# Gate logits of the last three token groups as TensorE products instead of sixteen VectorE multiply-and-sums

## The chip, the cores and the metric

The kernel runs on one core of a Trainium2 chip. The metric is device time in microseconds (us), the median of several executions of the same compiled kernel; lower is better. Engines are named as in the profile: PE (TensorE products), PEld (TensorE weight loads), DVE (VectorE), ACT (ScalarE), POOL (GpSimd), SP (the engine that only issues DMAs here).

## The reference

Three stages, in float32. A recurrent attention over 768 steps gives 3072 rows of 320 numbers. A dense two-layer network (320 to 2048 to 320, leaky ReLU) turns each row into a new row. Then every row is sent to one of eight experts:

```python
logits = x @ w_gate                          # 3072 x 320 by 320 x 8
expert_idx = np.argmax(logits, axis=1)
probs = softmax(logits)                      # gate_w = the chosen expert's probability
for e in range(E):
    mask = expert_idx == e
    out[mask] = gate_w[mask, None] * (np.maximum(x[mask] @ w1[e], 0.0) @ w2[e])
```

## The kernel before

**Groups.** The 3072 rows go in 12 groups of 256 (two tiles of 128 rows), numbered 0 to 11. Attention works chunk by chunk; as soon as a group's rows are there, the dense network runs on them in 16 pairs of *halves*: the odd half of pair f is `layer1(f)` (8 products into a `psH` bank, then ACT `g`, DVE `g`, ACT `gh`), the even half is `layer2(f-2)` (6 products that add up in the two `psX` banks) followed by `close` (POOL `gl`, line 712). `layer2` of a pair needs that pair's `gl`. A written-out list of words (START, STEP, LATE, END, TAIL) sets the order of everything; H is one half. In TAIL only the dense network and the first expert's loads are left; then `go` (line 1127) runs the expert slots j = 0 to 15, each in eight steps f of `layer1` (8 products) and, two steps late, `layer2` (6 products).

**Routing of a group.** With the last `layer2` of a group, `take` copies its rows from `psX` to `X` (one buffer, line 739, ACT). The list that `route` (line 723) returns is then worked off, one entry per half: 16 entries `logits` (line 742, DVE, one multiply-and-sum over 128 x 320 for one expert and one tile), `first` and `second` (argmax), `third` (line 760: position products on PE, DVE reciprocal), `fourth` (line 772: SP writes both tiles of `X` to the DRAM tensor `x2d`, line 774), `fifth` with `place(0)` and three entries later `place(1)` (line 787: POOL scatters row numbers into the DRAM tables `tbl[0]`, `tbl[1]`). That is 28 entries after `take`. The routing of group 9 begins in END, that of group 10 in TAIL, that of group 11 with TAIL's last half and goes on in `go`, where PACE gives the number of entries in each step f: (2, 1) in slot 0, (3, 3) in slot 1, (2, 2) later. Behind it in the same list come the entries of `plan.make`, which decide the later slots.

**What reads the routing's results.** Slots 0 to 2 are chosen early. Their row numbers are loaded by `fetch` (line 1031, SP, `sid` from `tbl[0]` and `tbl[1]`; the loads for slots 0 and 1 both stand at the word i of TAIL), and POOL gathers the rows from `x2d` with them (line 1039), at the words t. The framework orders accesses to one DRAM tensor as it does tiles: a gather from `x2d` waits for all earlier writes to it, a write waits for earlier gathers, a load from `tbl` waits for earlier scatters, and a scatter waits for earlier loads. SP, POOL and PE work strictly in order. SP's list also holds the expert weights' loads (`raw`, lines 1017 and 1019, five pieces per slot into one buffer; a piece waits until the old one has been split by ACT and by DVE, or by POOL for slot 1, lines 1059 to 1069).

**Order of TAIL around the change**, with the half's number: 337 to 341, first `raw` pieces, i (sid loads), 342 to 344, `memset`, ..., 350, first gather, ..., 356 (`take` of group 10), ..., 360, second gather, ..., 363, third gather, ..., 376, fourth gather, ..., 386 (`take` of group 11). Group 9's `take` is in half 324.

**Banks.** In END `s.bank()` gives one of four `psA` banks; in TAIL one of the two `psH` banks, which `layer1` also uses; in `go` `layer1` goes round these two and one more (`eph`).

Of the kernel before, what the change touches and what calls it, by code (L numbers as in the profile page):

```python
# [11 lines left out]
F32 = mybir.dt.float32  # L12
# [14 lines left out]
DM = H * D  # L27
FF = 2048
NF = FF // 128
E, F2 = 8, 1024  # L30
SL = 256
CAP = NT + SL
NSLOT = NT // SL + E - 1
PACE = (2, 1), (3, 3), (2, 2)
FETCH = 1, 5
EARLY, NE = {9: (0, 1), 10: (2,)}, 3
LOAD, SPLIT = 18, 27
# [34 lines left out]
def layouts(r, k, v, w, a, b, moe_w_in, moe_w_out, moe2_w_gate, moe2_w1, moe2_w2):  # L72


    def pair(x):
        return x.reshape(B, 2, 4, NC, C, D).transpose(3, 1, 5, 0, 2, 4).reshape(NC, 2, D, 16, C)

    def pad(y):
        return np.ascontiguousarray(np.concatenate([y, y[:, :, :24]], axis=2).reshape(NC, 128, -1))

    def flat(x):
        return np.ascontiguousarray(x.reshape(B, 2, 4, NC, C, D).transpose(3, 5, 1, 0, 2, 4).reshape(NC, D, NU * C))

    def words(x):
        x = np.ascontiguousarray(x)
        return x.view(np.int64) if x.dtype == np.float64 else x

    pw = pair(w)
    hw = pad(np.concatenate([np.zeros(pw.shape[:-1] + (1,), pw.dtype), pw], axis=-1))
    hw = np.concatenate([hw, np.zeros(hw.shape[:2] + (2,), hw.dtype)], axis=-1)  # L90
    w1 = moe2_w1
    tail = w1[:, 256:320]
    hw1 = np.concatenate([w1[:, 0:128], w1[:, 128:256], np.concatenate([tail, tail], axis=1)], axis=2)
    hw2 = moe2_w2.reshape(E, 8, 128, DM).transpose(0, 2, 1, 3).reshape(E, 128, 8 * DM)
    wt = moe_w_in[256:320]
    return {
        "nr": r, "nk": k, "nv": v, "nw": w, "na": a, "nb": b,
        "h1": np.ascontiguousarray(np.concatenate([hw, pad(pair(a)), pad(np.concatenate([pair(k), pair(b)], axis=-1))], axis=2)),
        "hr": flat(r),
        "hvt": flat(v),  # L100
        "hv": np.ascontiguousarray(v.reshape(B, 2, 4, NC, C, D).transpose(3, 4, 1, 0, 2, 5).reshape(NC, C, NU * D)),
        "hwi": words(np.concatenate([moe_w_in[0:128], moe_w_in[128:256], np.concatenate([wt[:, 0:FF // 2], wt[:, FF // 2:]], axis=0)], axis=1)),
        "hwo": words(moe_w_out.reshape(NF, 128, DM).transpose(1, 0, 2).reshape(128, NF * DM)),
        "hwg": np.ascontiguousarray(moe2_w_gate.T),
        "hwe": np.ascontiguousarray(np.concatenate([hw1, hw2], axis=2)),
    }

# [19 lines left out]
def place(n):  # L127

    return 16 * (n // 16) + 8 * (n % 2) + n % 16 // 2
# [371 lines left out]
class Moe1:  # L501
# [170 lines left out]
    def rows(s, g):  # L672

        x = s.x2d.rearrange("(b n) d -> b (n d)", b=B)[:, 2 * C * g * XW:]
        s.nc.sync.dma_start(x.rearrange("b (q f) -> q b f", q=120), s.wis[0:120, None, 0:616].bitcast(F32).to_broadcast([120, B, 616]))

    def load_x(s, src):
        nc = s.nc
        s.xr = s.p2.tile([128, 3, 256], F32R, name="xl", tag="xl")
        x = s.xr.bitcast(F32)  # L680
        nc.sync.dma_start(x[:, 0:2, :], src[0:256].rearrange("(k p) t -> p k t", p=128))
        nc.sync.dma_start(x[0:64, 2, :], src[256:320])
        nc.sync.dma_start(x[64:128, 2, :], src[256:320])
# [36 lines left out]
            for n, (x, w) in enumerate(((gh, s.woh), (gh, s.wol), (gl, s.woh))):  # L720
                nc.tensor.matmul(s.x2[t][:, 0:DM], x[:, o], w[:, f, :], start=(f == 0 and n == 0), stop=(f == NF - 1 and n == 2))  # L721

    def route(s, dest, ids):

        nc = s.nc
        X = s.r1.tile([128, 2, XW], F32, name="X2", tag="X2")
        lg = s.r2.tile([128, 2, E], F32, name="lg")
        sm = s.r2.tile([128, 2, 4], F32, name="sm")
        wk = s.r2.tile([128, 2, E], F32, name="wk")
        oh = s.r2.tile([128, 2, E], BF16, name="oh")  # L730
        dst = s.r2.tile([128, 2], I32, name="dst")
        bc = lambda x: x.to_broadcast([128, 2, E])
        code = s.code[:, None, :].to_broadcast([128, 2, E])
        box = {}
        x2 = s.x2

        def take():
            for t in range(2):
                nc.scalar.copy(out=X[:, t, 0:DM], in_=x2[t][:, 0:DM])  # L739

        def logits(e, t):
            nc.vector.scalar_tensor_tensor(  # L742
                out=s.junk, in0=X[:, t, 0:DM], scalar=1.0, in1=s.wg[:, e], op0=ALU.mult, op1=ALU.mult, accum_out=lg[:, t, e:e + 1])

        def rest():
            pass

        def first():
            nc.vector.tensor_reduce(out=sm[:, :, 0], in_=lg, axis=AX.X, op=ALU.max)
            nc.vector.tensor_tensor(out=wk, in0=lg, in1=bc(sm[:, :, 0:1]), op=ALU.is_equal)  # L750
            nc.vector.tensor_tensor(out=lg, in0=lg, in1=bc(sm[:, :, 0:1]), op=ALU.subtract)
            nc.scalar.activation(out=lg, in_=lg, func=AF.Exp)
            nc.scalar.copy(out=X[:, :, DM:DM + 64], in_=X[:, :, DM - 64:DM])

        def second():
            nc.vector.tensor_tensor(out=wk, in0=wk, in1=code, op=ALU.mult)
            nc.vector.tensor_reduce(out=sm[:, :, 1], in_=wk, axis=AX.X, op=ALU.max)
            nc.vector.tensor_tensor(out=oh, in0=code, in1=bc(sm[:, :, 1:2]), op=ALU.is_equal)

        def third():  # L760
            nc.vector.tensor_reduce(out=sm[:, :, 2], in_=lg, axis=AX.X, op=ALU.add)
            ps = box["ps"] = s.bank()
            for t in range(2):
                o = ps[:, E * t:E * t + E]
                nc.tensor.matmul(o, s.tri, oh[:, t, :], start=True, stop=False)
                if t:
                    nc.tensor.matmul(o, s.ones, oh[:, 0, :], start=False, stop=False)
                nc.tensor.matmul(o, s.ones, s.run, start=False, stop=True)
            nc.vector.tensor_scalar_add(out=sm[:, :, 2], in0=sm[:, :, 2], scalar1=1e-9)
            nc.vector.reciprocal(out=X[:, :, DM + 64], in_=sm[:, :, 2])  # L770

        def fourth():
            for t in range(2):
                nc.sync.dma_start(dest[t], X[:, t, :])
            nc.vector.tensor_tensor(
                out=wk, in0=box["ps"][:, 0:2 * E].rearrange("p (t e) -> p t e", t=2), in1=s.ecap[:, None, :].to_broadcast([128, 2, E]), op=ALU.add)
            nc.vector.tensor_tensor(out=wk, in0=wk, in1=oh, op=ALU.mult)
            nc.vector.tensor_reduce(out=sm[:, :, 3], in_=wk, axis=AX.X, op=ALU.add)
            nc.vector.tensor_copy(dst, sm[:, :, 3])

        def fifth():
            for t in range(2):
                nc.vector.tensor_tensor(out=s.run, in0=s.run, in1=oh[:, t, :], op=ALU.add)
            place(0)

        def place(t):
            nc.gpsimd.indirect_dma_start(
                out=s.tbl[t], out_offset=bass.IndirectOffsetOnAxis(ap=dst[:, t:t + 1], axis=0), in_=ids[:, t:t + 1], in_offset=None,
                bounds_check=NTB - 1, oob_is_err=False)

        return [take] + [lambda e=e, t=t: logits(e, t) for e in range(E) for t in range(2)] + [first, rest, second, rest, rest, rest, third, fourth, fifth, rest, rest, lambda: place(1)]

    def units(s):

        lag = []

        def second():
            g, f, gh, gl = lag.pop(0)
            s.layer2(f, gh, gl)
            if f == NF - 1:  # L800
                r = s.route([s.x2c[2 * g], s.x2c[2 * g + 1]], s.ids[:, 2 * g:2 * g + 2])
                r.pop(0)()
                return r
            return []

        for g in range(NC // 2):
            for f in range(NF):
                *a, close = s.layer1(f)
                lag.append((g, f, *a))
                yield []  # L810
                r = second() if len(lag) > 2 else []
                close()
                yield r
        while lag:
            yield second()
# [155 lines left out]
class Moe2:  # L971
# [155 lines left out]
    def go(s, ready, finish):  # L1127
# [3 lines left out]
        def step(n):  # L1131
            for _ in range(n):
                if ready:
                    ready.pop(0)()
                elif next(finish, True):
                    return False
            return True

        for j in range(NFIX):
            sp = s.split(j + 1, s.nc.gpsimd if j == 0 else None) if j + 1 < NFIX else []  # L1140
            ld = []
            for f in range(8):
                lag.append((j, f, *s.layer1(j, f)))
                if sp:
                    sp.pop(0)()
                step(PACE[min(j, 2)][0])
                if len(lag) > 2:
                    s.layer2(*lag.pop(0))
                if sp and f % 3 != 2:
                    sp.pop(0)()  # L1150
                step(PACE[min(j, 2)][1])
                if f == 1 and j + 2 < NFIX:
# [94 lines left out]
def overlap(tc, at, m1, plan):  # L1247

    nc = tc.nc
# [36 lines left out]
    def half():  # L1286
# [10 lines left out]
        if done == 2 * NF:  # L1297
            for _ in ws:
                pass
            m1.rows(9)  # L1300
        g = done // (2 * NF)
        new = next(units, None)
        if new is None:
# [116 lines left out]
```

## Time and profile before

| | us |
|---|---|
| median of 3 executions | 1122.68 (1119.37 to 1127.97) |
| the profiled execution's own time | 1121.85 |
| its span in the trace | 1120.1 |
| PE busy in the span | 953.4 (85%) |
| DVE busy in the span | 820.3 (73%) |

The time lies 1.75 us above the span, and the profiled execution 0.83 us below the median. Times in the text are us from the span's start. A busy share is a mean over stages: the table says nothing yet on which engine sets the end.

### The profile page before, as it was taken

The page shows a single profiled execution, that of the slowest core. Times are in us where ns is not written, and L with a number is a line of the kernel's source. Part 1 is how long each engine was busy: PE and PEld are TensorE (multiplying, and loading weights), DVE is VectorE, ACT ScalarE, POOL GpSimd, SP SyncE. Part 2 cuts the span into 40 slices and gives each one's busy share as a digit, 9 for nine tenths or more (in the row PEclk, how much of TensorE's full clock was granted, in tenths as well). Part 3 has the DMA queues.
Part 4 walks back from the last instruction along what each step waited for, and adds up shares of the span by engine and source line. Part 5 has one row for each costly group of instructions (what it writes and reads, how often), then busy time and mean ns, then how long its engine had stood idle before and what let it go on. Part 6 is the DMA issues. An engine that isn't in the chain of part 4 may idle for free. (4 is left out here: it accounts for less than half of the span.)

```text
span 1120.1 us, 40696 instructions
## 1 busy us (share of the span) xinstructions
PE 953.4 (85%) x16817; PEld 897.7 (80%) x16817; DVE 820.3 (73%) x1946; ACT 527.8 (47%) x1308; POOL 503.2 (45%) x690
## 2 busy tenths in 40 slices
PE   3476778978799899999899999999787799999993
PEld 3366676868788888888788888999777799999992
DVE  8989787757778777868786777676569677777760
ACT  4455454653344344444444344444444466666640
POOL 5123144215863498338843783334537123233220
PEclk9999986878999999999999999999898899999997
DMA  7878776855546654565645342334235653741620
GB/s 248 238 220 224 215 197 175 226 149 153 147 133 165 145 160 138 162 157 162 151 135 144 91 90 76 102 89 134 54 83 160 138 168 113 231 117 58 190 78 11
DMA packets 132379, 163.18 MB, mean 146 GB/s; under 512 B 67708, under 2 KB 89868, under 8 KB 132056
## 3 DMA queue, kind: packets, MB, share of 16 engines
q1 hardware_dynamic: 122071, 141.30, 46.7%
q10 hardware_dynamic: 5760, 10.49, 3.2%
q0 software_dynamic: 4352, 8.69, 2.6%
q8 instruction: 135, 2.21, 0.9%
q14 instruction: 61, 0.49, 0.2%
HBM read 127.61 MB, written 42.27 MB: 152 GB/s over the span
## 5 line engine op out<-in xcount | busy, mean ns | idle before, releaser
L712 POOL TENSOR_TENSOR gl<-g,gh 128x256 fp32r<-128x256 f32 x192 | 155.2, 811 | 224.5 <-ACT gh L711 194.2
L710 DVE TENSOR_TENSOR g<-psH,g 128x256 f32<-128x256 f32 x192 | 81.1, 423 | 117.1 <-ACT g L709 110.5
L711 ACT CAST gh<-g 128x256 fp32r<-128x256 f32 x192 | 77.9, 406 | 165.7 <-DVE g L710 158.1
L721 PE MATMUL psX<-woh,gl 128*128 128x320 f32 x384 | 125.1, 326 | 12.4 <-POOL gl L712 11.9
L721 PE MATMUL psX<-woh,gh 128*128 128x320 f32 x384 | 133.6, 348 | 1.2 <-ACT woh L638 1.1
L709 ACT ACTIVATE g<-psH 128x256 f32<-128x256 f32 x192 | 73.7, 384 | 119.5 <-PE psH L705 89.0
L721 PE MATMUL psX<-wol,gh 128*128 128x320 f32 x384 | 123.2, 321 | 0.2 <-issue 0.2
L742 DVE SCALAR_TENSOR_TENSOR junk<-X,raws 128x320 bf16<-128x320 f32 x192 | 113.6, 591 | 11.5 <-ACT X L739 9.0
L259 PE MATMUL psA<-AtI,KB 40*64 40x72 f32 x1408 | 72.1, 266 | 37.9 <-DVE KB L238 18.7
L259 PEld LDWEIGHTS psA<-AtI,KB 40*64 40x64 f32 x1408 | 63.9, 169 | 44.4 <-POOL woh L237 18.6
L1123 POOL DMA_INDIRECT out<-ey,sid x32 | 34.5, 1078 | 122.9 <-ACT ey L1122 63.2
L705 PE MATMUL psH<-xh,wih 128*128 128x256 f32 x384 | 86.8, 309 | 3.3 <-DVE g L710 2.9
L721 PEld LDWEIGHTS psX<-woh,gl 128*128 128x128 f32 x384 | 76.4, 199 | 15.8 <-POOL gl L712 15.7
L721 PEld LDWEIGHTS psX<-woh,gh 128*128 128x128 f32 x384 | 76.3, 199 | 7.3 <-ACT gh L711 1.5
L299 POOL TENSOR_TENSOR itmp<-Tinv 128x30 f32<-128x30 f32 (+14 forms) x120 | 69.9, 582 | 26.3 <-DVE Tinv L291 19.1
L705 PE MATMUL psH<-xl,wih 128*128 128x256 f32 x384 | 81.0, 294 | 0.3 <-DVE xl L690 0.3
L705 PE MATMUL psH<-xh,wil 128*128 128x256 f32 x384 | 80.5, 293 | 0.0
L721 PEld LDWEIGHTS psX<-wol,gh 128*128 128x128 f32 x384 | 76.6, 200 | 0.7 <-issue 0.4
L305 POOL TENSOR_TENSOR Tinv<-Tinv,itmp 128x30 f32<-128x30 f32 (+14 forms) x120 | 73.4, 611 | 7.8
L705 PEld LDWEIGHTS psH<-xh,wih 128*128 128x128 f32 x384 | 66.3, 200 | 8.3 <-DVE g L710 5.6
L705 PEld LDWEIGHTS psH<-xl,wih 128*128 128x128 f32 x384 | 63.3, 202 | 0.6 <-DVE xl L690 0.6
L1101 DVE SCALAR_TENSOR_TENSOR ehl<-psH,ehh 128x256 fp32r<-128x256 f32 x86 | 36.1, 420 | 37.7 <-ACT ehh L1100 34.9
(278 smaller groups left out, 2762.7 us busy)
## 6 DMA issues: line engine op xcount, KB each, us to landing
raw<-hwe SPq DMA_DIRECT2D x48, 512.0 KB
raw<-hwe SPq DMA_DIRECT2D x32, 640.0 KB
in<-h SPq DMA_DIRECT2D x23, 521.0 KB
KB<-h SPq DMA_DIRECT2D x22, 512.0 KB
L<-dKBr SPq DMA_DIRECT2D x24, 320.0 KB
dKBr<-KBr SPq DMA_DIRECT2D x22, 320.0 KB
lamY<-dl SPq DMA_DIRECT2D x24, 264.0 KB
dl<-lam SPq DMA_DIRECT2D x22, 264.0 KB
```

The costliest lines, as they stand in the source:

```text
L259: nc.tensor.matmul(v[64 * i:64 * i + 64, k, :], z["KB"][64 * i:64 * i + 40, p, :], z["AtI"][64 * i:64 * i + 40, p, :], start=True, stop=True)
L299: eng.tensor_tensor(out=box["v"], in0=T[:, k + 1:32, k:k + 1].to_broadcast([128, n, k]), in1=T[:, k:k + 1, 0:k].to_broadcast([128, n, k]), ...
L305: eng.tensor_tensor(out=T[:, k + 1:32, 0:k], in0=T[:, k + 1:32, 0:k], in1=box["v"], op=ALU.add)
L705: nc.tensor.matmul(ps[:, 0:256], w, x, start=(n == 0), stop=(n == 7))
L709: nc.scalar.activation(out=g, in_=ps[:, 0:256], func=AF.Copy, scale=0.01)
L710: nc.vector.tensor_tensor(out=g, in0=ps[:, 0:256], in1=g, op=ALU.max)
L711: nc.scalar.copy(out=gh, in_=g)
L712: return gh, gl, lambda: nc.gpsimd.tensor_tensor(out=gl, in0=g, in1=gh, op=ALU.subtract)
L721: nc.tensor.matmul(s.x2[t][:, 0:DM], x[:, o], w[:, f, :], start=(f == 0 and n == 0), stop=(f == NF - 1 and n == 2))
L742: nc.vector.scalar_tensor_tensor(out=s.junk, in0=X[:, t, 0:DM], scalar=1.0, in1=s.wg[:, e], op0=ALU.mult, op1=ALU.mult, accum_out=lg[:, t, ...
L1101: nc.vector.scalar_tensor_tensor(out=hl, in0=ps, scalar=0.0, in1=hh, op0=ALU.max, op1=ALU.subtract)
L1123: nc.gpsimd.indirect_dma_start(out=s.out, out_offset=bass.IndirectOffsetOnAxis(ap=ids[:, t:t + 1], axis=0), in_=y[:, t, :], in_offset=None ...
```

## The change

Groups 9, 10 and 11 get their logits otherwise. `turn(t)` transposes the three column blocks of a tile of `X` on PE (columns 0, 128 and 192 on; the rows of the gate's weights that would count twice are zero) into a bank, ACT copies them to SBUF; `product(t)` multiplies them with the gate's weights in three float32 products into eight columns of the same bank, and ACT copies these to `lg`. The six entries `turn`, `rest`, `product` for two tiles replace sixteen, and two more `rest` stand ahead of `third`: 20 entries in place of 28. `fourth` is entry 16 instead of 24, `fifth` 17 instead of 25, `place(1)` 20 instead of 28. A new load of the gate's weights stands behind `rows(9)` in SP's list, and slot 1's PACE is (2, 2).

```diff
-PACE = (2, 1), (3, 3), (2, 2)
+PACE = (2, 1), (2, 2), (2, 2)
+TURNED = 9
...
+    gate = np.zeros((128, 3, E), np.float32)
+    gate[:, 0], gate[:, 1], gate[64:, 2] = moe2_w_gate[0:128], moe2_w_gate[128:256], moe2_w_gate[256:320]
...
+    def late(s):
+
+        s.gate = s.none.bitcast(F32)[:, 0:3 * E].rearrange("p (n e) -> p n e", n=3)
+        s.nc.sync.dma_start(s.gate, s.i["hwt"])
+        s.wT = s.raws.bitcast(F32)[:, 0:2, 0:384]
...
+        def turn(t):
+            ps = box[t] = s.bank()
+            for n, a in enumerate((0, 128, DM - 128)):
+                nc.tensor.transpose(ps[:, 128 * n:128 * n + 128], X[:, t, a:a + 128], s.k.ident)
+            nc.scalar.copy(out=s.wT[:, t], in_=ps[:, 0:384])
+
+        def product(t):
+            o = box[t][:, 0:E]
+            for n in range(3):
+                nc.tensor.matmul(o, s.wT[:, t, 128 * n:128 * n + 128], s.gate[:, n, :], start=n == 0, stop=n == 2)
+            nc.scalar.copy(out=lg[:, t], in_=o)
...
-        return [take] + [lambda e=e, t=t: logits(e, t) for e in range(E) for t in range(2)] + [first, rest, second, rest, rest, rest, third, fourth, fifth, rest, rest, lambda: place(1)]
+        if turned:
+            by = [lambda: turn(0), rest, lambda: product(0), lambda: turn(1), rest, lambda: product(1)]
+        else:
+            by = [lambda e=e, t=t: logits(e, t) for e in range(E) for t in range(2)]
+        return [take] + by + [first, rest, second] + [rest] * (5 if turned else 3) + [third, fourth, fifth, rest, rest, lambda: place(1)]
...
             m1.rows(9)
+            m1.late()
```

## Rows read from the trace of the kernel before

**Rows 1.** Busy time by stage: stretch, length, busy us (instructions), granted clock, DMA share, GB/s.
```profile
750.00:800.00 50.00, 42.36 (x564) 39.89 (x552) 30.65 (x115) 20.95 (x54) 21.20 (x25) 0.94 0.39 105
800.00:850.00 50.00, 42.54 (x294) 39.42 (x293) 37.05 (x99) 24.66 (x58) 27.01 (x29) 0.96 0.37 92
850.00:900.00 50.00, 39.59 (x271) 38.83 (x270) 37.86 (x90) 21.09 (x46) 19.85 (x18) 0.86 0.58 130
900.00:950.00 50.00, 50.00 (x387) 49.98 (x386) 37.02 (x65) 31.60 (x66) 14.16 (x16) 1.00 0.50 149
```

**Rows 2.** PE's waits from 740 to 900: us in total, times, longest.
```profile
PE psX L721 <- POOL gl L712: 6.6, 2, 6.5
PE epy L1113 <- ACT ey L1122: 5.5, 1, 5.5
PE psH L765 <- DVE ehl L1101: 4.4, 1, 4.4
PE eph L1097 <- ACT X L739: 3.9, 1, 3.9
```

**Rows 3.** Timeline of all engines around group 9's take: start, us, what.
```profile
756.07 0.31 PE L721 MATMUL psX<-woh,gl 128*128 128x320 f32 x1
...
758.33 0.75 ACT L739 COPY X<-psX 128x320 f32<-128x320 f32 x2
```

**Rows 4.** POOL's timeline in TAIL; in brackets idle before and releaser.
```profile
774.83 1.02 POOL L712 TENSOR_TENSOR gl<-g,gh 128x256 fp32r<-128x256 f32 x1 [0.82 <-ACT gh L711]
...
794.60 1.04 POOL L1039 DMA_INDIRECT xg<-x2d,sid  x1 [6.53 <-issue]
...
815.43 0.74 POOL L712 TENSOR_TENSOR gl<-g,gh 128x256 fp32r<-128x256 f32 x1 [0.27 <-ACT gh L711]
...
822.96 1.01 POOL L1039 DMA_INDIRECT xg<-x2d,sid  x1
```

**Rows 5.** SP's timeline from 735 to 910, the issues of row numbers and of x2d.
```profile
776.34 2.52 SPq L1031 DMA_DIRECT2D sid<-tbl  x4
...
782.24 1.32 SPq L774 DMA_DIRECT2D x2d<-X  x2
...
826.21 1.14 SPq L774 DMA_DIRECT2D x2d<-X  x2
...
843.60 0.90 SPq L1031 DMA_DIRECT2D sid<-tbl  x2
```

**Rows 6.** PE's timeline at the end of its longest wait.
```profile
797.79 0.63 PE L721 MATMUL psX<-woh,gl 128*128 128x320 f32 x1 [6.46 <-POOL gl L712]
```

**Rows 7.** DMA issues from 740 to 900: engine, count, median us to landing where shown.
```profile
xg<-x2d,sid POOLq DMA_INDIRECT x10, 3.1
tbl<-ids,dst POOLq DMA_INDIRECT x8, 16.9
```

**Rows 8.** Cost of a transpose and of a float32 product: PE's timeline, two places.
```profile
765.30 1.42 PE L475 MATMUL psA<-Rr,L 104*40 104x32 f32 x64
...
827.90 0.82 PE L1080 MATMUL epx<-ident,xg 128*128 128x128 f32 x6
```

**Rows 9.** Line 742 from 830 to 860: ns min/median/max, first and last start.
```profile
L742 DVE SCALAR_TENSOR_TENSOR junk<-X,raws x16: 480/492/1464, 837.8 to 851.8; 128x320 bf16<-128x320 f32 x16
```

**Rows 10.** Timeline of all engines over the first expert slot.
```profile
831.47 0.31 PE L721 MATMUL psX<-woh,gl 128*128 128x320 f32 x1
...
837.36 0.76 ACT L739 COPY X<-psX 128x320 f32<-128x320 f32 x2 [5.96 <-DMA x2d<-X]
...
839.60 5.80 POOL L1060 TENSOR_TENSOR bl<-raw,bh 128x512 fp32r<-128x512 f32 x4 [8.73 <-ACT bh L1059]
...
857.70 0.17 PE L765 MATMUL psH<-oh,tri 128*128 128x8 bf16 x1 [4.36 <-DVE ehl L1101]
...
859.58 0.84 PE L1097 MATMUL eph<-bxh,bh 128*128 128x256 f32 x3
```

**Rows 11.** The same timeline where slot 1's rows go out.
```profile
881.56 0.98 POOL L1123 DMA_INDIRECT out<-ey,sid  x1 [15.05 <-DMA out<-ey,sid]
...
887.74 0.63 PE L1113 MATMUL epy<-ah,ehh 128*128 128x320 f32 x1 [5.47 <-ACT ey L1122]
```

More of the change, by code (lines that the diff above doesn't have):

```diff
@@ L104, in layouts @@
         "hwg": np.ascontiguousarray(moe2_w_gate.T),
+        "hwt": gate,
         "hwe": np.ascontiguousarray(np.concatenate([hw1, hw2], axis=2)),
@@ L721, in layer2, with route @@
                 nc.tensor.matmul(s.x2[t][:, 0:DM], x[:, o], w[:, f, :], start=(f == 0 and n == 0), stop=(f == NF - 1 and n == 2))
-    def route(s, dest, ids):
+    def route(s, dest, ids, turned=False):
         nc = s.nc
@@ L800, in second @@
             if f == NF - 1:
-                r = s.route([s.x2c[2 * g], s.x2c[2 * g + 1]], s.ids[:, 2 * g:2 * g + 2])
+                r = s.route([s.x2c[2 * g], s.x2c[2 * g + 1]], s.ids[:, 2 * g:2 * g + 2], g >= TURNED)
                 r.pop(0)()
```

## The prediction

> **What bounds the kernel now.** I read the stages first [rows 1]. From 900 on PE is busy all the time at full clock, 387 instructions in 50 us, 0.129 us each: there the end is set by products alone, and whatever PE loses or wins before 900 moves the end by as much. From 750 to 900 it is idle for 25.5 of 150 us, and all three routings that change lie there. The clock costs more: 800 to 850 has 294 instructions, 37.9 us at 0.129, for which it took 42.54; 850 to 900 has 271, 35.0 us, in 39.59. So 4.6 us are lost to the half clock in each. Second I read PE's waits there [rows 2]: four hold 20.4 us, for POOL, for the output rows, for DVE and for `X`. Last I followed each one to its release.
>
> The first ends at 797.79 after 6.46 us, so PE stopped at 791.33 [rows 6]. POOL stood at a gather from 788.07 to 794.60 [rows 4]; no releaser is shown, but the gather reads `x2d`, whose write was issued at 782.24 [rows 5], so that write took about 12.4 us. The second write, issued at 826.21 [rows 5], held ACT's `take` until 837.36 [rows 10], 11.1 us, and PE lost 3.9 [rows 2]. The third wait ends at 857.70 with the position products [rows 10]; the sixteen sums of line 742 fill DVE ahead of them from 837.8 to 851.8, up to 1464 ns each where POOL works beside them, against 492 [rows 9]. The fourth, 5.47, is slot 1's output buffer: its second scatter stood 15.05 us for the landing of the first [rows 11].
>
> **Part 1, group 9 in END (loss 4.0).** The sums here have cover: PE is nearly full, so their removal is worth nothing. `turn(0)` follows the last `layer2` on PE, which ends at 756.38, but needs the first copy of `X`, ready at about 758.7 [rows 3]: PE waits 2.3 us, with the next `layer1` and attention's transposes queued behind. Six transposes cost 0.82 [rows 8]. A float32 product runs as two passes; 64 passes with 40 weight columns took 1.42 [rows 8], 22 ns each, scaled to 128 columns 71 ns, so twelve cost 0.85; bounds 0.27 (unscaled) and 1.55 (0.129 each). Together 1.7 per group, an estimate, with no cover where PE is full. ACT's four small copies are covered: it is busy 21 to 25 us in 50 [rows 1]. The gate's load is one issue on SP eight groups earlier, under 0.7 us (half of an `x2d` pair [rows 5]), with attention's products as its cover; I take nothing. PACE (2, 2) leaves 44 entries for 24 places in slot 0 and 4 a step in slot 1, done by its fifth step as before: nothing.
>
> **Part 2, group 9's tables (loss 2.7).** Everything behind the logits comes eight halves earlier, and passes the word i. Before, the row-number loads of slots 0 and 1 stood ahead of group 9's scatters. Now `place(0)` (half 340) stands ahead of them and `place(1)` (half 343) behind: the loads wait for the first scatter to land, POOL waits for the loads, and `gl` of half 344 queues behind POOL. Meanwhile the old gather wait goes, since `x2d` is written early. `third` moves to half 338, whose close was at 774.83 [rows 4]: `x2d` goes at about 774.9 and lands 11.1 to 12.4 later, near 787. `place(0)` goes about 777.7 (one pair of halves, 14 products, 1.81 us, and the DVE steps). Its landing is between 3.1 us, a gather's, and 16.9, the one table write that shows it [rows 7]. I take 9.3: like the 16.9 it follows close behind an `x2d` write, and I let it land with that. That is 787.0. Four loads take 2.5 us to issue [rows 5] and the last some 2 to land (at most 3.1): `place(1)` starts at 791.4, PE goes on 1.85 later (3.19 before, less one DMA instruction and its gap), at 793.3. PE stops four pairs earlier than before, at 791.33 - 7.24 = 784.1. So 9.2 us idle in place of 6.46. With the ends, 3.0 and 16.8: a win of 3.5 to a loss of 10.3.
>
> The Trainium skill, page "DMA: Bandwidth & Descriptors", section "Queues, rings and completion order", states that a DMA's semaphore update lands only after every earlier write of the same DMA engine, across its queues. By that the scatter cannot be told before the `x2d` write in front of it, and part 2 is the loss above; by the gather's 3.1 it would be a win, the sum 6.2 us less. The 16.9 agrees with the rule.
>
> **Part 3, group 10 in TAIL (loss 5.7).** The same 1.7 of PE, a wait of `turn(0)` for `X`, between 0 and the 2.3 of END, taken as 1.2 because ACT is less loaded, and waits for the two `psH` banks, which a turn holds for two halves: 0 to 2, taken as 0.6. That is 3.5. Then `x2d` (from half 379 to 371) passes the fourth gather (376), which must now wait for it: close of half 370 at 815.43 [rows 4], landing 826.6 or later; POOL reached that gather at 822.96 [rows 4]. PE holds out 3.26 us (788.07 to 791.33), to 826.2, and goes on after gather and `gl` at 828.4: 2.2 lost (0 to 8). SP gains here: the second to fourth `raw` pieces stood behind the late `x2d` write; now they move into DMA time that was free.
>
> **Part 4, group 11 and slot 0 (win 9.6).** `x2d` of group 10 is long down, so `take` no longer waits. From the last `layer2` (831.78) to slot 1's first product (859.58) it took 27.8 us [rows 10]. Now: 100 products at 0.129, 12.9; the transposes of slot 1's rows 0.8; turns and gate products 1.7; waits for `X`, banks and evacuation in the first three steps 2.5 and in the others 1.6, both estimates. That is 19.5, a win of 8.3. The small steps of the routing stay on DVE, POOL's split starts earlier. Past 859.58 the clock recovered: some 1.3 of the 4.6 us come back.
>
> **Part 5, slot 1's output (win 5.5).** All of slot 0 moves 9 us ahead, and group 11's `x2d` write further still, out of the way of the first output scatter. With a landing of about 10 us in place of 15, the second scatter lands when PE needs the buffer. Of 5.47 I take 4.0, and 1.5 of clock; bounds 0 and 7.8. Late next: the same scatters in slot 2, which steady state covers.
>
> **Sum.** 4.0 + 2.7 + 5.7 = 12.4 lost, 9.6 + 5.5 = 15.1 won: 2.7 us faster. Against the profiled execution's 1121.85 (span 1120.1, 1.75 around it) that is 1119.2; that execution lies 0.83 below the median.
>
> **Rivals.** *The tables land quickly* (0.17): 3.1 us as a gather, no waits in parts 2 and 3, part 5 whole. Lost 4.0 + 3.5 - 3.5, won 9.6 + 7.8: 1108.5. For it: nothing else is in those tables' way; against it the 16.9.
> *POOL's wait at `place(1)` is long* (0.18): 16.9 to land, the extra stop 10.3, part 5 nothing because scatters stay slow. Lost 4.0 + 10.3 + 5.7, won 9.6: 10.4 slower, 1132.2. It decides from where `place(1)` starts after 794.1, 2.7 later than I think. For it: the `raw` pieces are issued right behind that `x2d` write, so DMA is full.
> *POOL's split sets slot 0, not DVE* (0.17), so that the sums' removal frees nothing: POOL began 2.24 after ACT's `take` and PE reached slot 1 20.0 later [rows 10]; from 833.1 plus 2.2 that gives 855.3, a win of 4.3 in place of 8.3, so 1123.2. Against it: POOL's operations were slowed by those very sums.
>
> **How the numbers follow.** The forecast has 0.48 and 1114 to 1126 as its own range. About 1% is what a measurement tells from no change: below 1110.6 or above 1133.1. Faster by more takes most of the first rival and a bit of the forecast's edge, 0.17; slower most of the second with part 3's upper bound, 0.14; within, 0.69. The range goes from just under the first rival to the second, 1107 to 1133.
>
> **What would show it.** Right: line 787's second scatter of group 9 waits on POOL 8 to 12 us near 780 to 792 and PE idles 9 there; the wait at the first gather is gone, a short one stands at the fourth; ACT's `take` of group 11 does not wait; slot 1 starts about 20 us after the last `layer2`; PE's wait for the output buffer is under 2. Wrong: PE idle from 750 to 900 at 12 or less (first rival), or a stop over 14 us in TAIL (second). If PE has idle time past 900, the claim that all of it counts one to one fails.

## The result, and the profile after

The changed kernel takes 1132.07 us (median of 20 runs, 1124.39 to 1139.23) against 1126.33 of the kernel before measured beside it (20 runs, 1119.11 to 1133.64): a ratio of 1.0064, 95% interval 1.0041 to 1.0087. (Ratios, here and below, leave out the few executions in a slower state.) It is slower by 5.7 us by the medians and some 7 by the ratio, where 2.7 us of gain were forecast; the time lies in the range given (1107 to 1133), at its end, and outside the forecast's own (1114 to 1126). The profiled execution after has a span of 1129.1, 9.0 more than before; that is one execution of each kernel, and the one of before (1121.85) lies 4.5 us below the median of the 20 runs.

Where the 9.0 us arise is seen by following PE through both traces. Times are counted from the end of group 8's last `layer2` (711.90 before, 711.31 after), which the change does not touch.

| PE reaches | before | after | difference |
|---|---|---|---|
| second write of `xT` in END (SP) | 55.8 | 62.4 | +6.5 |
| end of group 10's last `layer2` | 87.3 | 99.3 | +11.9 |
| end of group 11's last `layer2` | 119.9 | 133.5 | +13.7 |
| slot 1, first product | 147.7 | 151.4 | +3.7 |
| slot 2, first product | 165.2 | 171.9 | +6.7 |
| slot 3, first product | 188.6 | 198.3 | +9.7 |
| last product | 388.7 | 398.4 | +9.7 |

From slot 3 on nothing changes any more: what is lost before 900 arrives whole at the end, as the stage rows of before said it would [rows 1]. The same stages after (length, busy us of PE, PEld, DVE, ACT, POOL, granted clock, DMA share, GB/s):

```profile
750.00:800.00 50.00, 37.58 (x504) 35.20 (x505) 18.49 (x75) 16.72 (x44) 12.30 (x17) 0.85 0.30 89
800.00:850.00 50.00, 46.47 (x334) 44.76 (x334) 20.70 (x48) 26.57 (x66) 24.77 (x32) 0.94 0.30 73
850.00:900.00 50.00, 36.36 (x264) 34.68 (x265) 33.78 (x75) 21.55 (x47) 23.10 (x20) 0.91 0.66 150
900.00:950.00 50.00, 50.00 (x383) 49.97 (x383) 37.31 (x65) 32.26 (x66) 15.30 (x18) 0.99 0.53 162
```

DVE's relief is there: 18.5 and 20.7 us busy in the first two stages where it had 30.7 and 37.1. PE gained in the second (46.5 in place of 42.5) and lost in the first and third. Its waits from 740 to 900 (total, times, longest) stand beside [rows 2]:

```profile
PE psX L731 <- POOL gl L722: 10.9, 2, 9.4
PE epy L1139 <- ACT ey L1148: 9.0, 1, 9.0
PE epy L1139 <- DVE ehl L1127: 4.1, 4, 2.0
PE psA L758 <- ACT X L749: 2.4, 1, 2.4
PE psH L758 <- ACT X L749: 1.3, 2, 0.9
```

The wait for `X` at group 11 (3.9) and the one for the position products (4.4) are down to 0.4 and 0.5. The stop behind POOL's `gl` grew from 6.5 to 9.4, the one at slot 1's output rows from 5.5 to 9.0, and a wait for `X` at the first `turn` is new. PE's timeline has the ends of the two long stops (before: [rows 6, 11]) and the new wait with what follows it:

```profile
758.22 0.90 PE L758 MATMUL psA<-ident,X 128*128 128x128 f32 x3 [2.44 <-ACT X L749]
...
764.49 0.91 PE L764 MATMUL psA<-none,raws 128*128 128x8 f32 x6
...
799.60 0.64 PE L731 MATMUL psX<-woh,gl 128*128 128x320 f32 x1 [9.39 <-POOL gl L722]
...
897.48 0.64 PE L1139 MATMUL epy<-ah,ehh 128*128 128x320 f32 x1 [9.04 <-ACT ey L1148]
```

PE alone in END after (length, PE busy, granted clock, DMA share, GB/s); before, the clock stood at 1.00 in all of these:

```profile
755.00:760.00 5.00, 2.56 (x15) 0.80 0.03 8
760.00:765.00 5.00, 5.00 (x34) 0.51 0.06 20
765.00:770.00 5.00, 5.00 (x159) 1.00 0.08 27
```

POOL's timeline after has both long stops in it (before: [rows 4, 10, 11]):

```profile
784.32 0.98 POOL L809 DMA_INDIRECT tbl<-ids,dst  x1 [0.30 <-DVE run L805]
...
797.80 0.99 POOL L809 DMA_INDIRECT tbl<-ids,dst  x1 [11.58 <-DMA sid<-tbl]
...
847.82 5.18 POOL L1086 TENSOR_TENSOR bl<-raw,bh 128x512 fp32r<-128x512 f32 x4 [4.07 <-ACT lg L765]
...
861.50 2.56 POOL L1090 TENSOR_TENSOR bh<-raw,bh 64x512 fp32r<-64x512 f32 x2 [3.80 <-issue]
864.14 8.03 POOL L1095 TENSOR_TENSOR bl<-raw,bh 128x640 fp32r<-128x640 f32 x4
872.33 1.30 POOL L809 DMA_INDIRECT tbl<-ids,dst  x1 [0.16 <-issue]
873.93 1.14 POOL L809 DMA_INDIRECT tbl<-ids,dst  x1 [0.30 <-issue]
875.38 1.03 POOL L1149 DMA_INDIRECT out<-ey,sid  x1 [0.30 <-issue]
890.49 0.98 POOL L1149 DMA_INDIRECT out<-ey,sid  x1 [14.08 <-DVE bl L1086]
```

The first two rows are group 9's tables: the second scatter stands 11.58 us for the row-number loads, which SP could issue only when the first had landed:

```profile
781.11 1.30 SPq L796 DMA_DIRECT2D x2d<-X  x2
...
793.17 2.51 SPq L1057 DMA_DIRECT2D sid<-tbl  x4
```

The rest is one chain of work and landings. POOL splits slot 1's weights from 847.82 to 872.2, with a stop for the landing of slot 2's gathers (the 3.80; the profile names no releaser, but in the program that instruction waits for POOL's earlier DMAs, and the gathers land at 861.1). Only then come group 11's table scatters, and behind them the first output scatter. It lands near 889.7. The second names DVE as its releaser, but DVE's `ey` was done at 873.6: where the engine named has long been done, it is a DMA, here the landing of the first. When the second has landed, at 896.8, ACT may overwrite `ey`, and PE goes on at 897.48. So slot 0's shorter work on PE met an output chain that starts with POOL's split and did not shrink with it: from the split's start to the first output scatter it took 27.6 us, before 25.9.

### The profile page after: what moved, and what is told of

The parts are those of the page before. It is cut to its first block, busy times and chain, and to the rows that moved or that the text cites. A ratio compares the mean times of both kernels' runs of the same rounds, so it can differ in the third digit from the quotient of the medians.

```text
span 1129.1 us, 40727 instructions
## 1 busy us (share of the span) xinstructions
PE 954.2 (85%) x16871; PEld 899.6 (80%) x16871; DVE 794.8 (70%) x1850; ACT 531.1 (47%) x1320; POOL 498.9 (44%) x690
## 5 line engine op out<-in xcount | busy, mean ns | idle before, releaser
L722 POOL TENSOR_TENSOR gl<-g,gh 128x256 fp32r<-128x256 f32 x192 | 152.1, 795 | 234.6 <-ACT gh L721 210.9
L752 DVE SCALAR_TENSOR_TENSOR junk<-X,raws 128x320 bf16<-128x320 f32 x144 | 83.2, 578 | 4.1 <-ACT X L749 2.3
L1127 DVE SCALAR_TENSOR_TENSOR ehl<-psH,ehh 128x256 fp32r<-128x256 f32 x86 | 36.2, 420 | 42.5 <-ACT ehh L1126 39.8
```

What stands on the lines that cost most here:

```text
L722: return gh, gl, lambda: nc.gpsimd.tensor_tensor(out=gl, in0=g, in1=gh, op=ALU.subtract)
L752: nc.vector.scalar_tensor_tensor(out=s.junk, in0=X[:, t, 0:DM], scalar=1.0, in1=s.wg[:, e], op0=ALU.mult, op1=ALU.mult, accum_out=lg[:, t, ...
L1127: nc.vector.scalar_tensor_tensor(out=hl, in0=ps, scalar=0.0, in1=hh, op0=ALU.max, op1=ALU.subtract)
```

## Experiments

**Theory.** The end is set by this chain on POOL: split, tables, first output scatter, its landing, second scatter, PE's stall. Whatever slot 0 wins ahead of it on PE only lengthens the stall. The stop in TAIL is the order of tables and row-number loads. **Rivals:** the pieces of `raw` fill the DMA engines, so that scatters land late whatever stands ahead of them; the single `ey` buffer is the price; the wait at the first `turn` and the half clock are the main loss.

**e1_eleven: only group 11 turned.**
```diff
-TURNED = 9
+TURNED = 11
```


> Only group 11's logits are PE products; groups 9 and 10 go back to the sums, PACE stays as in the changed kernel. Theory (POOL's chain in slot 0 sets slot 1's output: split of the next weights, group 11's scatters, first output scatter, its landing, second scatter, PE's stall at the output buffer): that chain starts when ACT's copy of X is let go by group 10's row write, as in the kernel before, so slot 0 gets some 8 us shorter on PE but the stall of 5.47 us at the output buffer grows by about as much, and the time is that of before, ratio to before 0.998 to 1.002 (1124 to 1129 us). Rival (the sums on DVE set the pace of slot 0 and PE's gain counts one to one): ratio 0.992 to 0.994, 1117 to 1120 us.

Ratio 0.9973 (0.9949 to 0.9997). Between the two, nearer to the theory: in the profile, from group 8 to the last product it takes 388.5, as before (388.7), although the sums of slot 0 are gone. But not by the theory's way: slot 0 is no shorter (27.7 us, before 27.8), since group 11's copy still waits for group 10's rows (5.6 us), and PE's wait for the output rows is 4.2, less than before.

**e2_later: all turns two halves later.**
```diff
-by = [lambda: turn(0), rest, lambda: product(0), ...
+by = [rest, rest, lambda: turn(0), rest, lambda: product(0), ...
-... [first, rest, second] + [rest] * (5 if turned else 3) + [third, ...
+... [first, rest, second] + [rest] * 3 + [third, ...
```


> The first turn of each turned group comes two halves later (two of the five rests in front of it), all else of the order in place. Theory (PE's 2.4 us wait for X at the turn in group 9, and the half clock right after it, are paid because the turn follows the copy too closely): the wait is under 0.3 us, the granted clock in 755 to 765 stays at 1.0, group 10's last layer2 ends 3 to 4 us earlier, and the end moves by as much: ratio to before about 1.003, 1128 to 1129.5 us. Rival (it is the transposes themselves, or what stands behind them, that lower the clock): wait gone but clock still 0.5 to 0.8, less than 2 us of gain, ratio 1.005 to 1.007.

Ratio 0.9997 (0.9968 to 1.0026): more than expected, and not from where the theory had it. The wait for `X` at the turn is gone, but the clock falls all the same (0.88 in 760 to 765, 0.50 in 765 to 770). Group 10 ended only 2.9 us earlier, slot 1 started 2.5 later than in the changed kernel, and then there was no wait for the output rows at all: 13.3 us won by slot 3. The tables had left at 864.54 and 865.88, the output scatter at 870.32 landed in 8.4 us.

**e3_dve: slot 1's weight split on DVE.**
```diff
-sp = s.split(j + 1, s.nc.gpsimd if j == 0 else None) if ...
+sp = s.split(j + 1) if ...
```


> The changed kernel with slot 1's weight split on DVE in place of POOL (ten subtractions, some 7.4 us of DVE at 0.69 to 0.81 us). Theory (POOL's chain): the first output scatter goes near 867 in place of 875.4, the second near 881 in place of 890.5, PE's wait of 9.04 us for the output rows falls to under 1.5, ratio to before 0.997 to 1.000, some 7 to 9 us under the changed kernel. Rival 1 (the raw pieces fill the DMA engines, so an earlier scatter lands as late): the wait stays over 6 us, ratio 1.004 to 1.007. Rival 2 (DVE becomes the bound in slot 0): slot 0 grows by 3 us or more and the ratio is 1.002 or above.

Ratio 1.0011 (0.9980 to 1.0042), some 6 us under the changed kernel. The wait for the output rows is gone, as the theory has it; but slot 0 is 2.0 us longer and a wait of 2.7 for ACT is new, so rival 2 has a share.

**e4_ey: three output-row buffers.**
```diff
-y = s.p1.tile([128, 2, DM], F32, name="ey")
+y = s.p3.tile([128, 2, DM], F32, name="ey")
```


> The changed kernel with three output-row buffers in place of one (ey from the pool of three). Theory (the 9.04 us stall at slot 1's output is the buffer's, held by the landing of the first scatters): PE's wait for ey is gone, no other wait over 2 us takes its place, ratio to before 0.998 to 1.000, 7 to 9 us under the changed kernel. Rival (the scatters are only late because the transfers are, and something else in slot 1 or 2, the next gathers or weights behind the same landings, is late next): at least half of the 9 us turns up as another wait, ratio 1.002 to 1.006.

Ratio 1.0089 (1.0055 to 1.0123): a miss. PE's wait for `ey` is gone, but another took its place (PE's waits, 740 to 915):

```profile
PE epx L1106 <- DMA xg<-x2d,sid: 5.3, 2, 4.5
```

POOL still holds its second output scatter until the first has landed (12.03 us), because the framework orders two writes to `out`, and slot 3's gathers stand behind it on POOL. The buffer was not the price; the landing is.

**f1_notables: group 11's table scatters left out.**
```diff
-            place(0)
+            if turned != 11:
+                place(0)
...
-... rest, rest, lambda: place(1)]
+... rest, rest, rest if turned == 11 else lambda: place(1)]
```


> The changed kernel without group 11's two table scatters (left out, so the last 256 tokens are in no table; all other work stays). In the changed kernel they leave POOL at 872.33 and 873.93, close ahead of the first output scatter at 875.38, the second lands near 888 and the output scatter near 890. Theory (the output scatter lands late because it stands behind the two table scatters): it lands within 9 us, the second output scatter waits under 9 in place of 14.08, PE's wait of 9.04 for the output rows is under 2, ratio to before 0.997 to 1.001. Rival (the pieces of raw fill the DMA engines, tables or not): landing 12 us or more, wait over 6, ratio 1.004 to 1.008.

Ratio 0.9976 (0.9948 to 1.0004), as the theory expected. POOL's split ends as late as in the changed kernel, but now the second output scatter stands 5.48 in place of 14.08:

```profile
867.86 7.65 POOL L1096 TENSOR_TENSOR bl<-raw,bh 128x640 fp32r<-128x640 f32 x4
875.66 1.30 POOL L1150 DMA_INDIRECT out<-ey,sid  x1 [0.16 <-issue]
882.44 1.00 POOL L1150 DMA_INDIRECT out<-ey,sid  x1 [5.48 <-DVE tf L990]
```

PE has no wait for the output rows. The pieces of `raw` are the same in both, so they alone do not make the landing 14 us long. By its semaphore updates the first scatter landed 6.0 us after its issue here; in the changed kernel slot 1's first, at 900.37, took 2.6. What the rest comes from, no run separates.

**f2_later_tail: later turns in groups 9 and 10 only** (group 11 as changed).
```diff
+        if turned in (9, 10):
+            return [take, rest, rest] + by + [first, rest, second, rest, rest, rest, third, fourth, fifth, rest, rest, lambda: place(1)]
```


> The turns come two halves later in groups 9 and 10 only; group 11, in slot 0, as in the changed kernel. Theory (the later turns are worth 3 to 4 us up to the end of group 11, from the wait for X and the clock behind it; the rest of what the variant with all turns later won came from a slot 0 of another pace, whose output scatter did not follow close on the table scatters): the wait for the output rows is still 6 to 10 us, ratio to before 1.003 to 1.005. Rival (groups 9 and 10 are the cause of all of it): no wait for the output rows over 2, ratio 0.999 to 1.001.

Ratio 1.0072 (1.0047 to 1.0097), above the range expected: the wait for the output rows is still 7.8 and nothing is won. The later turn has no wait for `X`, but the clock falls all the same, later in the stage:

```profile
765.00:770.00 5.00, 2.84 (x137) 0.96 0.13 44
770.00:775.00 5.00, 5.00 (x82) 0.70 0.02 3
```

To the second `xT` write it loses 5.0 us to the kernel before, in place of 6.5. Against e2_later only group 11's order differs, so e2_later's gain came from slot 0.

**f3_apart: the same, with the rows' write early and the tables where they were.**
```diff
-... third, fourth, fifth, rest, rest, lambda: place(1)]
+... third, fourth] + [rest] * 8 + [fifth, rest, rest, lambda: place(1)]
```


> As the kernel with later turns in groups 9 and 10, and there the rows' write stays early (as in the changed kernel) while the table scatters go back to where they stood before (eight rests between them). Theory (the 9.4 us stop in TAIL is the second table scatter's wait for the row-number loads behind the first scatter; the 6.46 of before is the late row write): both are under 1 us, group 10's last layer2 ends 8 to 11 us earlier than in the changed kernel; what of it arrives at the end depends on the wait for the output rows: 1116 to 1121 us, ratio 0.994 to 0.999. Rival (the gather or the scatters wait for other transfers there, whatever the order): a stop of 5 us or more remains in 780 to 805, ratio 1.000 to 1.004.

Ratio 0.9973 (0.9947 to 0.9999), as the theory expected. Against f2_later_tail the tables' order alone is changed, and that is worth 1.0% (0.9973 to 1.0072). PE's waits, 740 to 915:

```profile
PE epy L1141 <- ACT ey L1150: 6.8, 1, 6.8
PE epy L1141 <- DVE ehl L1129: 2.8, 2, 2.0
PE psX L731 <- POOL gl L722: 2.6, 2, 1.5
```

The stop of 9.4 in TAIL is gone without the 6.5 of before coming back; group 10 ends 10.5 us earlier than in the changed kernel.

**f4_apart_all: and group 11 later as well**, as in e2_later.

> The same with group 11's turns later as well (slot 0 as in the variant with all turns later). Theory (that slot 0 sends its tables early enough ahead of the output scatter): no wait for the output rows, and the freed stop in TAIL arrives whole: ratio to before 0.989 to 0.993, 1108 to 1113 us. Rival (slot 0 and 1 wait for transfers that do not move with PE: weights, tables, gathers): slot 1 or 2 gets a new wait of 4 us or more, ratio 0.996 to 1.000.

Ratio 0.9969 (0.9945 to 0.9992): the rival, level with f3_apart. The tables left at 864.54 and 866.55, the output scatter at 868.59, close behind, and PE waited 4.4. Turning later in slot 0 does not of itself set the tables well ahead; in e2_later it happened to.

**g1_after_out: f3_apart, with group 11's tables between slot 0's two output scatters.**
```diff
+LAST = []
...
-            place(0)
+            if turned != 11:
+                place(0)
...
+... (lambda: LAST.extend([lambda: place(0), lambda: place(1)])) if turned == 11 else lambda: place(1)]
...  # behind the output scatter in layer2 of the experts
+                while LAST:
+                    LAST.pop(0)()
```


> The kernel with early rows and late tables (f3_apart), and group 11's two table scatters stand on POOL between the first and the second output scatter of slot 0, in place of ahead of both. Theory (an output scatter lands late when table scatters stand close ahead of it): the first lands within 9 us, some 4 us earlier than the 12.3 it took there; the second may pay part of it, so PE's wait of 6.8 us for the output rows falls to 1 to 4: ratio to before 0.992 to 0.996. Rival (the cost only moves: the second scatter lands late in place of the first, or slot 3's row numbers, read from those tables, come late for its gathers): a wait of 5 us or more stays, ratio 0.996 to 1.000.

Ratio 0.9932 (0.9905 to 0.9959), as the theory expected: the first scatter leaves at 862.54 and the second at 869.03, so the landing took at most 6.5 us with no table ahead; PE's wait is 2.9. Part of the cost moved, as the rival had it: the second scatter, now behind the tables, landed 11.8 us after its issue, at 880.9, and PE's 2.9 us end behind it.

**g2_two: f3_apart, with the last four subtractions of the split on DVE.**
```diff
             nc.scalar.copy(out=h2[:, a:a + 640], in_=x)
-            eng.tensor_tensor(out=l2[:, a:a + 640], ...
+            nc.vector.tensor_tensor(out=l2[:, a:a + 640], ...
```


> The kernel with early rows and late tables (f3_apart), with the last four subtractions of slot 1's weight split on DVE (0.81 us each there) in place of POOL (1.9 us each). Theory (POOL's split holds back the tables, and these the output scatter): the tables leave near 857 in place of 863, over 5 us ahead of the output scatter, which lands within 9 us in place of 12.3; PE's wait of 6.8 falls under 2, ratio to before 0.990 to 0.994, 1111 to 1115 us. Rival (the split on DVE delays the position products or the plan, or the landing is as long): slot 0 longer by 2 us or more or a wait of 5 us left, ratio 0.996 to 1.000.

Ratio 0.9913 (0.9881 to 0.9944), 1111.85 us: as expected in time, but the landing is still long:

```profile
855.71 1.03 POOL L809 DMA_INDIRECT tbl<-ids,dst  x1 [0.28 <-POOL bh L1092]
857.05 0.99 POOL L809 DMA_INDIRECT tbl<-ids,dst  x1 [0.30 <-issue]
861.14 1.12 POOL L1151 DMA_INDIRECT out<-ey,sid  x1 [3.10 <-ACT ey L1150]
874.39 0.97 POOL L1151 DMA_INDIRECT out<-ey,sid  x1 [12.14 <-DMA out<-ey,sid]
```

With the tables 4.1 us ahead it takes 13 us, no less than the 12 of f3_apart. What helps is that the scatter leaves earlier (861.14; 866.28 in f3_apart), when `ey` is ready and not when POOL is; the rows have landed before PE needs their buffer, and it has no wait for them.

**g3_two_all: the same in f4_apart_all.**

> The same four subtractions on DVE, in the kernel whose group 11 also turns later (f4_apart_all). Theory: its wait of 4.4 us for the output rows goes, ratio to before 0.991 to 0.995, level with the one whose group 11 turns at once. Rival (slot 0's slower start there, some 5 us longer to slot 1, counts once the wait is gone): 0.995 to 0.998, slower than the other by 3 us or more.

Ratio 0.9928 (0.9898 to 0.9958): the theory's range; the interval does not part it from g2_two.

**h1_before_two: the kernel before, with the four subtractions on DVE.**

> The kernel before (sums on DVE) with the last four subtractions of slot 1's split on DVE in place of POOL. Theory (there it is DVE's chain of sums and routing that holds the tables: DVE gives the rows' places at 861.8, POOL sends the tables at 862.2): 3.2 us more on DVE ahead of the routing, the tables leave no earlier, the wait of 5.47 us for the output rows stays over 4, ratio to before 0.999 to 1.003. Rival (POOL's split alone held them, with or without the sums): the wait goes, ratio 0.993 to 0.996.

Ratio 0.9939 (0.9907 to 0.9971): the rival. DVE does hold the tables (POOL waits 7.02 us for DVE and sends them 0.5 us earlier than before, counted from group 8). But the wait for the output rows falls from 5.47 to 1.5, since slot 1 is reached 1.7 later and the output scatter now stands 5.0 us behind the tables in place of 2.0 and lands within 11.5. So the kernel before was held by the same output chain, and one line mends most of it there.

**h2_after_two: the changed kernel with them on DVE.**

> The changed kernel with those four subtractions on DVE. Theory (POOL holds the tables there, 9.04 us of wait follow from it): the wait for the output rows under 3 us, ratio to before 0.997 to 1.001, 6 us or more under the changed kernel; the 9.4 us stop in TAIL stays. Rival (only the earlier start of the tail made it work in the other variant): wait over 5, ratio 1.003 or above.

Ratio 0.9983 (0.9947 to 1.0019), as the theory expected: no wait for the output rows, and the stop in TAIL stays (10.3). A wait of 4.1 for DVE in slot 0 is new.

**h3_two_at_once: g2_two with groups 9 and 10 turning at once again.**
```diff
-            return [take, rest, rest] + by + [first, rest, second, rest, rest, rest, third, fourth] + ...
+            return [take] + by + [first, rest, second, rest, rest, rest, rest, rest, third, fourth] + ...
```


> The fastest variant so far (g2_two) with its turns in groups 9 and 10 at once again, as in the changed kernel (the two rests go behind). Theory (the wait for X and the half clock behind it cost some 3 us, which the wait for the output rows swallowed in the variant that only turned later): with that wait gone they arrive: ratio to before 0.993 to 0.995, PE's wait for X of 2.4 us or more back. Rival (they are given back anyway, by a stop that stands there with or without them): ratio 0.990 to 0.992.

Ratio 0.9909 (0.9875 to 0.9944): the rival. The wait for `X` of 2.5 is back, and group 10 ends as early as in g2_two (88.0 and 88.3 from group 8). The wait at the turn shows no loss of its own here: to the second `xT` write both lose 5 us to the kernel before (5.1 and 5.0).

**i1_eleven_two: e1_eleven with the four subtractions on DVE.**

> Only group 11's logits as PE products (as in e1_eleven), and the last four subtractions of slot 1's split on DVE. It tells what turning groups 9 and 10 is worth once the output rows are no longer waited for. Theory (with the tables put back in their old order, turning 9 and 10 takes away the late row writes: the 6.5 us stop at the gather and the 5.6 us wait of group 11's copy, less some 5 us of turns): this kernel has both waits and no wait for the output rows over 2, ratio to before 0.992 to 0.996, above g2_two and h3_two_at_once. Rival (turning 9 and 10 gives as much as it costs): ratio 0.989 to 0.992, level with them.

Ratio 0.9968 (0.9935 to 1.0001), just above the theory's range. It has the stop at the gather (6.6) and group 11's wait for `X` (5.9), and none for the output rows. Its interval overlaps those of h1_before_two and h3_two_at_once: that turning groups 9 and 10 is worth something with the tables put back is the likelier reading (in the profile 5.7 us to the last product against h3), but not settled by the times.

g2_two and h3_two_at_once are the fastest, 0.9% under the kernel before and some 1.5% under the changed one. The kernel before with the four subtractions moved (h1) is 0.6% under, with an interval that overlaps theirs.

## Why the prediction was wrong

| part | forecast | measured (from the table above) |
|---|---|---|
| 1, group 9 in END | 4.0 lost | 6.5 lost |
| 2, group 9's tables | 2.7 lost | 5.4 lost (11.9 - 6.5) |
| 3, group 10 | 5.7 lost | 1.7 lost (13.7 - 11.9) |
| 4, slot 0 | 9.6 won | 9.9 won (27.8 to 17.9) |
| 5, slot 1's output | 5.5 won | 6.0 lost (40.9 to 46.9, slot 1 to slot 3) |

**Part 5 is the step that failed**, 11.5 us off. It said "All of slot 0 moves 9 us ahead" and took from that that the output scatter would be early against PE's need. Slot 0 did get shorter, but as its start had moved 13.7 back, slot 1 began 3.7 later, and POOL's chain did not shrink with PE's work: its split began 2.25 us after slot 0's first product and, held by ACT's copies, slot 2's gathers and its own slower subtractions, let the first output scatter go at 875.38 in place of 865.53, 10.4 later as the table counts. The landing was 14.3, nearer to the 15 of [rows 11] than to the 10 taken: the reason given, group 11's `x2d` write out of the way, was not the one. In the changed kernel that write was down at 868.8, before the scatter left, and the scatter still landed late; without the two tables (f1) it landed within 6.8, with them behind it (g1) within 6.5. (In the kernel before, the write, the second table scatter and the output scatter landed together, at 880.4, 880.4 and 880.8, so there they can't be told apart.) The stall is not all of the 6.0: it grew by 3.6, and slot 1 ahead of it was 3.0 longer. There PE waited 4.1 us for DVE's `ehl` (the low-order part of the hidden values, which `layer2` needs), in place of 0.6; the prediction has no term for that. POOL's timeline of before has the chain too, in rows that the prediction did not take up:

```profile
853.17 2.50 POOL L1064 TENSOR_TENSOR bh<-raw,bh 64x512 fp32r<-64x512 f32 x2 [3.25 <-issue]
855.74 6.13 POOL L1069 TENSOR_TENSOR bl<-raw,bh 128x640 fp32r<-128x640 f32 x4
862.18 1.03 POOL L787 DMA_INDIRECT tbl<-ids,dst  x1 [0.31 <-DVE run L783]
863.52 1.15 POOL L787 DMA_INDIRECT tbl<-ids,dst  x1 [0.30 <-issue]
865.53 0.98 POOL L1123 DMA_INDIRECT out<-ey,sid  x1 [0.86 <-ACT ey L1122]
```

The rival of POOL's split priced it by slot 0's length, where it did not decide; its place was one step further on, at the output.

**Part 1** was too low by 2.5. The wait for `X` was as forecast (2.44 for 2.3), but the clock was left out: 0.51 in 760 to 765, most of it at the lower of its two levels, where before it stood at 1.00. Without the wait (f2) the clock falls a little later. How long it stays low differs between executions: where group 9 turns at once (the changed kernel, e3, e4, f1, h2, h3) the second `xT` write comes 5.1 to 9.0 us later than before, where it turns later (e2, f2, f3, f4, g1, g2, g3) 4.6 to 6.7, and in e1, where it does not turn but the clock fell too (0.88 and 0.77 in 750 to 760), 1.2. So the later turn may win something in END, but the times do not show it: f2 is level with the changed kernel, g2 with h3.

**Part 2** had its stop right. Moved by END's 6.5, `place(1)` at 791.4 and PE's going on at 793.3 become 797.9 and 799.8; the trace has 797.80 and 799.60, and 9.4 idle for 9.2. The first scatter took 8.85 us to let the loads go (784.32 to 793.17; taken were 9.3). That this term fitted was luck: it was taken as landing together with the `x2d` write, 11 to 12 us behind that one's issue, but by the semaphore updates the write was down at 788.7, 7.6 us behind its issue, and the scatter 4.4 us later. Of the other 2.5, some 1.5 are products at half clock behind the stop (0.71 in 800 to 810, where before had 0.95), an estimate from 6.2 us of them in place of 3.1; the last 1.0 is not assigned. f3 shows the cause, the order of tables and loads, by taking it away.

**Part 3** was too high: the wait for the fourth gather cost 1.5, and the turns found room (a wait for `X` of 0.9, none for a bank).

**Part 4** was right, in its waits too: group 11's `take` had no wait.

**The reading of the clock** was wrong for one stage. With 0.96 granted in 800 to 850 [rows 1], some 4 of the 50 us were at half clock, which by estimate can cost 2 us, not 4.6. For 850 to 900 (0.86) the 4.6 can stand. No term of the sum hangs on the first.

**Rivals.** Quick tables did not come. The rival of a long wait at `place(1)` gave 1132.2, close to the 1132.07 measured, and "part 5 nothing because scatters stay slow" was half of what happened; but its stop was 9.4 and not the 16.8 behind its price, so its sum fits by other terms. That idle time past 900 would be none held.

## To carry to other kernels

Before work is taken from the busy engine of a stage, follow every in-order queue that feeds the stage's output to its last instruction: here POOL's queue, off PE's critical path in slot 0, set when the output left, and PE felt it two slots later. Where a transfer must land before a buffer comes free, see what stands ahead of it in the same queue: here it landed late behind two scatters of single words. Moving four subtractions to another engine gave 0.6% in the kernel before, where the change itself lost 0.6%. When steps are taken out of an order written by hand, put rests where the ones that write and read the same DRAM tensor would change places.

## What the runs showed of the hardware

**A scatter's landing depends on what was issued just ahead of it.** The first output scatter (128 rows of 320 numbers) landed within 6.8 us (f1) and 6.5 us (g1) with no table scatter ahead, and in 7.1 (h2, tables 8.4 us ahead), 8.4 (e2, 4.4 ahead), 10 (e3), 12 (e4, f3) to 14.3 (changed kernel, 1.45 ahead) behind them; the gap alone does not order these (g2: 4.1 ahead, 12 to 13). By the semaphore updates it landed behind the second table scatter in all fifteen traces that have the tables ahead: 0.3 to 1.9 us behind it in seven (888.1 and 889.7 in the changed kernel, 873.8 and 874.3 in e1, 891.9 and 892.2 in e4), 2.4 to 5.0 in the others. The Trainium skill, page "DMA: Bandwidth & Descriptors", section "Queues, rings and completion order", has a DMA's semaphore update land only after every earlier write of the same DMA engine; the order agrees with that in all of them. Why a second scatter of 128 single words itself takes 8.7 (e2) to 16.9 us (before) is open.

**Beside POOL's subtractions DVE's smallest instructions take as long as what is left of the subtraction.** Beside POOL's 128 x 640 subtractions, DVE's steps on eight numbers took up to 1.5 us; timelines of both after, and the first cast before, where no subtraction of POOL's ran:

```profile
862.81 1.27 DVE L957 CAST ci<-cn 1x8 int32<-1x8 f32 x1
864.12 0.16 DVE L959 TENSOR_SCALAR ci<-ci 1x8 int32<-1x8 int32 x1
864.14 1.59 POOL L1095 TENSOR_TENSOR bl<-raw,bh 128x640 fp32r<-128x640 f32 x1
864.31 1.44 DVE L961 CAST cn<-ci 1x8 f32<-1x8 int32 x1
...
864.09 0.16 DVE L931 CAST ci<-cn 1x8 int32<-1x8 f32 x1
```

The second cast ends at 865.75, 0.02 us behind POOL's subtraction. POOL's own took 2.0 us each after and 1.6 before; after, DVE's 128 x 512 subtractions (line 1086) ran among them.

The Trainium skill, page "SBUF — State Buffer", section "SBUF: two separate sides", describes a port pair that VectorE and GpSimd hold in turns for a whole instruction. Casts that end with POOL's subtraction beside them, and take 0.16 without, agree with it.
